# The second feed-forward's three products as Strassen block products, on one core of a Trainium2

## The chip, the cores and the metric

The kernel runs on one core of a Trainium2 chip. The core has five engines with instruction queues of their own: PE (TensorE, matrix products), DVE (VectorE), ACT (ScalarE), POOL (GpSimd) and SP, which here issues all DMAs. PE writes its results to PSUM, which has eight banks of 512 float32 columns in 128 partitions; all else lies in SBUF, and the inputs, outputs and scratch of the kernel in DRAM. The metric is the device time of one execution in microseconds (us).

## The reference

Attention over 4 sequences of 576 tokens with 8 heads gives 2304 tokens of width 512. Two feed-forwards follow; the change is in the second.

```python
def _moe_ref(x, w_in, w_out):            # 512 -> 2048 -> 512
    h = x @ w_in
    g = h * np.cos(h)
    return (g @ w_out).astype(np.float32)

def _moe2_ref(x, w1, w2, w3, w_out):     # 512 -> 768 -> 512
    h = np.maximum(np.maximum(x @ w1, x @ w2), x @ w3)
    return (h @ w_out).astype(np.float32)
```

The weights of both feed-forwards arrive as 8-byte floats.

## The kernel before

The tokens stand in the free dimension and the features in the partitions. Each float32 operand is split into a high and a low half of type float32r, and a product is three matmuls (`PASSES`: high by high, low by high, high by low), each with a 128 by 128 stationary weight and up to 512 token columns. Tokens go in blocks of 512, 512, 512, 512 and 256.

The weights pass four steps: a DMA of the 8-byte words (`w_load`), a correction of the exponent on ACT (`w_exponent`, L177), two integer instructions on DVE that make the float32 bits (`w_bits`, L183 and L186), and the two halves (`w_halves`: L140 on ACT or DVE for the high one, L196 on POOL or DVE for the low one).

The first part of the program does the attention of the first block. Then come 80 steps of the first feed-forward, 16 for each block. A step has 12 matmuls of the first product (L346, inside `h_chunks`), 12 of the second (L389, inside `acc_chunk`), the chain for h cos h on DVE and ACT (L362 or L360, L366, L369, L205, L378, and then the halves L140 or L136 and L380), and a share of the next block's attention. The product alternates between two PSUM banks, so the matmuls of step s + 2 wait until L378 of step s has read its bank. The block's result goes through DRAM (`x1d`).

The second feed-forward has 30 steps (`ff2_h`, `ff2_acc`), 6 for each block. A step has three products of 12 matmuls (L346), of which DVE keeps the running maximum (L434, then L436 twice, each reading one PSUM bank), the halves of the maximum (L438 on ACT, L439 on DVE) and 12 matmuls of the output product (L389). Its tokens come back from `x1d` through `x1_raw` and are split again into a ring of 1536 columns (`x1_split`, L418 on ACT and L419 on DVE). Its 24 weight tiles of 128 by 512 are loaded and made ready in the last steps of the first feed-forward and the first ones of the second.

The Python order is not the engines' order. The tile layer places the instructions on each engine by costs of its own, and adds the semaphore waits; what it has placed is executed strictly in that order on each engine. Buffers are named tags of pools with a fixed number of copies, and a copy is free again when its last reader is done.

## Time and profile before

| | |
|---|---|
| median of 3 runs | 849.5 us (849.34 to 851.74) |
| profiled execution | 849.88 us, of which the span from first to last instruction 848.1 us |
| mean granted TensorE clock | 0.978 of full speed |
| busy share: PE, weight loads, DVE, ACT, POOL | 96%, 78%, 63%, 40%, 13% |
| second feed-forward, first to last matmul | 548.5 to 844.4 us |

A line of code names an instruction in the profile: L346 is the matmul of the hidden products of both feed-forwards, L389 that of both output products. "Busy" is the share of time in which an engine executed; a busy PE in this table is a stream of matmuls, not a peak rate. What to read first is how long PE runs without a gap, and in which stretches the other engines have time left.

### The profile page before, as it was taken

The page shows a single profiled execution, that of the slowest core. Times are in us where ns is not written, and L with a number is a line of the kernel's source. Part 1 is how long each engine was busy: PE and PEld are TensorE (multiplying, and loading weights), DVE is VectorE, ACT ScalarE, POOL GpSimd, SP SyncE. Part 2 cuts the span into 40 slices and gives each one's busy share as a digit, 9 for nine tenths or more (in the row PEclk, how much of TensorE's full clock was granted, in tenths as well). Part 3 has the DMA queues.
Part 4 walks back from the last instruction along what each step waited for, and adds up shares of the span by engine and source line. Part 5 has one row for each costly group of instructions (what it writes and reads, how often), then busy time and mean ns, then how long its engine had stood idle before and what let it go on. Part 6 is the DMA issues. An engine that isn't in the chain of part 4 may idle for free.

```text
span 848.1 us, 11770 instructions
## 1 busy us (share of the span) xinstructions
PE 816.0 (96%) x4358; PEld 659.8 (78%) x4358; DVE 530.3 (63%) x1376; ACT 341.7 (40%) x770; POOL 107.9 (13%) x96
## 2 busy tenths in 40 slices
PE   7858899999999999999999999999999999999998
PEld 6635677777777877777878889888888888888898
DVE  5888979658776678877665589995242242232232
ACT  5777877537663267673331246500020020010010
POOL 1454535310000000000000001230000000000000
PEclk9976989999999999999999999999999999999999
DMA  9953111102111021112200049400030020010010
GB/s 352 417 217 154 32 49 50 49 17 84 49 42 41 1 82 35 48 47 66 71 14 1 1 141 362 180 1 0 1 100 1 0 87 1 1 62 1 1 50 26
DMA packets 23818, 62.22 MB, mean 73 GB/s; under 512 B 2640, under 2 KB 4304, under 8 KB 23760
## 3 DMA queue, kind: packets, MB, share of 16 engines
q1 hardware_dynamic: 23760, 61.47, 20.6%
q8 instruction: 34, 0.56, 0.3%
q14 instruction: 24, 0.20, 0.1%
HBM read 52.02 MB, written 9.44 MB: 72 GB/s over the span
## 4 chain that ended last, share of the span: by engine, by line
PE 83%; DVE 7%; DMA 6%; issue 1%; ACT 1%; SPq 1%; POOL 0%; POOLq 0%; ACTq 0%
PE bank L346 47%; PE bank L389 30%; PE bank L256 3%; DMA w<-in_w_in 3%; PE bank L314 2%; DMA w<-in_w_out 2%; PE bank L303 1%; DVE wx L186 1%; DVE wx L183 1%; DVE r L369 1%; DVE gt L380 1%; DVE r L366 1%; DVE r L378 1%; DMA w<-in_w 1%; DVE e L263 0%
## 5 line engine op out<-in xcount | busy, mean ns | idle before, releaser
L346 PE MATMUL bank<-ring,w 128*128 128x512 f32 (+1 forms) x2040 | 465.4, 376 | 9.4 <-DVE r L378 7.1
L346 PEld LDWEIGHTS bank<-ring,w 128*128 128x128 f32 x2040 | 354.0, 190 | 78.1 <-DVE r L378 8.4
L389 PE MATMUL bank<-gt,w 128*128 128x512 f32 (+1 forms) x1320 | 303.5, 375 | 0.5 <-DVE gt L380 0.5
L389 PEld LDWEIGHTS bank<-gt,w 128*128 128x128 f32 x1320 | 229.6, 190 | 45.7 <-DVE gt L380 0.7
L438 ACT CAST gt<-mx 128x512 fp32r<-128x512 f32 (+1 forms) x30 | 17.3, 578 | 221.2 <-DVE mx L436 221.2
L205 ACT ACT_TABLE_LOAD x62 | 79.5, 1283 | 54.6 <-DVE r L369 45.8
L205 ACT ACTIVATE r<-r,hpi 128x512 f32<-128x512 f32 (+1 forms) x80 | 54.5, 681 | 114.6 <-DVE r L369 114.0
L436 DVE TENSOR_TENSOR mx<-bank,mx 128x512 f32<-128x512 f32 (+1 forms) x60 | 38.2, 637 | 88.5 <-PE bank L346 88.4
L205 ACT ACTIVATE e<-e,m 96x128 f32<-96x128 f32 x192 | 74.8, 391 | 7.1 <-DVE m L263 6.6
L196 POOL TENSOR_TENSOR w<-wx,w 128x512 fp32r<-128x512 f32 x44 | 63.4, 1447 | 111.7 <-ACT w L140 39.8
L378 DVE TENSOR_TENSOR r<-bank,r 128x512 f32<-128x512 f32 (+1 forms) x80 | 50.4, 631 | 22.2 <-ACT r L205 22.0
L434 DVE COPY mx<-bank 128x512 f32<-128x512 f32 (+1 forms) x30 | 19.1, 636 | 70.0 <-PE bank L346 70.0
L263 DVE CUSTOM_DVE_ANT_0 e<-bank,cs 96x128 f32<-96x128 f32 x192 | 45.1, 282 | 24.0 <-PE bank L256 11.8
L362 DVE TENSOR_SCALAR kk<-bank 128x512 int32<-128x512 f32 (+1 forms) x64 | 39.7, 621 | 28.7 <-PE bank L346 28.7
L366 DVE SCALAR_TENSOR_TENSOR r<-kk,bank 128x512 f32<-128x512 int32 (+1 forms) x80 | 50.3, 629 | 8.2 <-ACT kk L360 7.1
L136 POOL TENSOR_SCALAR gt<-r 128x512 fp32r<-128x512 f32 x24 | 15.2, 632 | 290.4 <-PE bank L389 238.0
L380 DVE TENSOR_TENSOR gt<-r,gt 128x512 fp32r<-128x512 f32 (+1 forms) x65 | 42.7, 658 | 13.5 <-POOL gt L136 10.3
L186 DVE SCALAR_TENSOR_TENSOR wx<-w,wx 128x512 int32<-128x512 int32 x56 | 44.8, 801 | 0.4
L256 PEld LDWEIGHTS bank<-qkv 64*96 64x96 f32 x288 | 24.2, 169 | 21.2 <-issue 9.5
L369 DVE TENSOR_SCALAR r<-r 128x512 f32<-128x512 f32 (+1 forms) x80 | 37.7, 471 | 0.9
L256 PE MATMUL bank<-qkv 64*96 64x128 f32 x288 | 34.7, 303 | 3.5 <-DVE m L263 2.6
L177 ACT ACTIVATE w<-w 128x512 f32<-128x512 f32 x56 | 36.2, 672 | 2.5 <-DMA w<-in_w_o 1.1
(37 smaller groups left out, 507.2 us busy)
## 6 DMA issues: line engine op xcount, KB each, us to landing
qkv<-in_qkv SPq DMA_DIRECT2D x36, 336.0 KB, 2.9
w<-in_w SPq DMA_DIRECT2D x18, 512.0 KB, 4.9
w<-in_w_in SPq DMA_DIRECT2D x16, 512.0 KB, 9.3
w<-in_w_out SPq DMA_DIRECT2D x16, 512.0 KB, 9.8
qkv<-in_qkv SPq DMA_DIRECT2D x12, 432.0 KB, 9.2
x1d<-o SPq DMA_DIRECT2D x16, 256.0 KB, 2.5
x1raw<-x1d SPq DMA_DIRECT2D x16, 256.0 KB, 2.8
outT<-o SPq DMA_DIRECT2D x16, 256.0 KB, 2.0
```

Of the source, the lines that this page charges most:

```text
L186: nc.vector.scalar_tensor_tensor(out=x, in0=low, scalar=29, in1=x, op0=ALU.logical_shift_right, op1=ALU.bitwise_or)
L196: tensor("w_lo").tensor_tensor(out=w[:, 1, :], in0=x, in1=w[:, 0, :].bitcast(F32), op=ALU.subtract)
L205: last_table.append(nc.scalar.activation(*args, **kw).ins)
L256: nc.tensor.matmul(sv, q[rows], k[rows], start=True, stop=True)
L263: nc.vector.tensor_tensor_reduce(out=e[:, 2 * j + h, :], in0=places_of[j, h], in1=mask[:, kind, :], scale=-1.0 / math.sqrt(D), scalar=3e38 ...
L346: nc.tensor.matmul(hv, w[:, a, 128 * c : 128 * c + 128], ring[c][:, x, c0 : c0 + n_tok], start=n == 0 and j == 0, stop=n == NC - 1 and j == 2,
L362: nc.vector.tensor_scalar(out=kk.bitcast(I32), in0=hv, scalar1=INV2PI, scalar2=0.25, op0=ALU.mult, op1=ALU.add)
L366: nc.vector.scalar_tensor_tensor(out=r, in0=kk.bitcast(I32), scalar=-2.0 * math.pi, in1=hv, op0=ALU.mult, op1=ALU.add)
L369: nc.vector.tensor_scalar(out=r, in0=r, scalar1=ARG_HI, scalar2=ARG_LO, op0=ALU.min, op1=ALU.max)
L378: nc.vector.tensor_tensor(out=r, in0=hv, in1=r, op=ALU.mult)
L380: tensor("g_lo").tensor_tensor(out=gt[:, 1, :], in0=r, in1=gt[:, 0, :].bitcast(F32), op=ALU.subtract)
L389: nc.tensor.matmul(a_dm, w[:, a, 128 * dm : 128 * dm + 128], gt[:, x, :], start=first and n == 0, stop=last and n == 2,)
```

## The change

The second feed-forward goes in three blocks of 768 tokens. Each of the three weight matrices is cut into three groups of 256 features, which makes nine "quads" for a block, numbered by feature group f and matrix j = 0, 1, 2. In a quad the 512 by 256 weight is a 2 by 2 matrix A of 256 by 256 blocks (feature half, input half), and the tokens are a 2 by 2 matrix B (input half, token half of 384). The four blocks of the result are made by Strassen's seven products in Winograd's form. A product is 2 chunks by 3 passes, 6 matmuls of 384 columns.

Four sums of A blocks (S1 to S4) are made on DVE for each quad and block (`a_sums`); A11, A12, A22 and the sums are then split, high half on ACT, low half on POOL (`a_direct`, `a_split`, `a_22`). Four sums of B blocks (T1 to T4) and the halves of B11, B21, B22 and the Ts are made once for each block on DVE and ACT (`b_make`). Four of the products are added in PSUM to an earlier one (`first` is False in `SUMS`); of three partial sums a copy is taken to SBUF on ACT between two products (`take`), and DVE adds the rest while it reads PSUM (`put`), and then takes the maximum over j, in SBUF.

The weights are no longer made ready in place. During the first feed-forward, 48 half tiles of 128 by 256 go through the DMA load, the exponent and the bits, and are stored as float32 in DRAM (`raw_piece`, `wd` and `wod`). Each quad of each block loads its 512 KB from `wd` again (`raw_load`). The output weights are loaded and split once, on ACT and DVE. The attention's inputs have 4 buffers instead of 5 (`RUNS`).

```diff
-AT2 = [RING - TB, 0, TB, RING - TB, 0]
+HALF = 384
+NB2 = NT // (2 * HALF)
+NQUAD = 3 * NF2 // 2
 LAG = 3
-RUNS = 5
...
+    cv = pool("cv", 2)
...
+    wd = drp.tile([NQUAD, 128, 2, 512], F32, name="wd")
+    wod = drp.tile([NF2 // 2, 128, 2, 512], F32, name="wod")
...
+        (dst[:, 256 * k : 256 * k + 256], w[:, 256 * k : 256 * k + 256]) for dst, w in halves2 for k in range(2)
+    ]
+    pieces2 = {}
+    def raw_piece(n):
+        if 0 <= n - 2 < len(halves2):
+            x = cv.tile([128, 256], I32, tag="c", name="cv")
+            bits(x, pieces2.pop(n - 2))
+            nc.sync.dma_start(out=halves2[n - 2][0], in_=x.bitcast(F32))
+        if 0 <= n - 1 < len(halves2):
+            exponent(pieces2[n - 1])
+        if 0 <= n < len(halves2):
+            w = wx.tile([128, 256], I64, tag="x", name="wh")
+            nc.sync.dma_start(out=w, in_=halves2[n][1])
+            pieces2[n] = w
...
+    QUADS = [(f, j) for f in range(NF2 // 2) for j in range(3)]
+    SUMS = {
+        1: ("X", "A11", "B11", True),
+        5: ("V", "S1", "T1", True),
+        2: ("Y", "A12", "B21", True),
+        6: ("X", "S2", "T2", False),
+        3: ("V", "S4", "B22", False),
+        7: ("X", "S3", "T3", False),
+        4: ("X", "A22", "T4", False),
+    }
...
+    def split(out, x, lo):
+        nc.scalar.copy(out[:, 0], x)
+        lo.tensor_tensor(out=out[:, 1], in0=x, in1=out[:, 0].bitcast(F32), op=ALU.subtract)
+    def raw_load(q):
+        if q < NB2 * NQUAD:
+            raws[q] = slot_tile(q % 3, [128, 2, 512], F32, "raw")
+            nc.sync.dma_start(out=raws[q], in_=wd[q % NQUAD])
+    def a_direct(q):
+        if q < NB2 * NQUAD:
+            ops[q] = {}
+            w = slot_tile(3 + q % 2 * 3, [128, 2, 512], F32R, "wa")
+            split(w, raws[q][:, 0], nc.gpsimd)
+            ops[q]["A11"], ops[q]["A12"] = w[:, :, :256], w[:, :, 256:]
+    def a_22(q):
+        if q < NB2 * NQUAD:
+            w = wx.tile([128, 2, 256], F32R, tag="x", name="w22")
+            split(w, raws.pop(q)[:, 1, 256:], nc.gpsimd)
+            ops[q]["A22"] = w
+    sums = {}
...
+                    sums[q] = slot_tile(9, [128, 4, 256], F32, "ws")
+                else:
+                    sums[q] = gp.tile([128, 4, 256], F32, tag="g", name="ws")
+                do = ((0, a21, a22, ALU.add), (1, sums[q][:, 0], a11, ALU.subtract))
+            else:
+                do = ((2, a11, a21, ALU.subtract), (3, a12, sums[q][:, 1], ALU.subtract))
+            for k, x, y, op in do:
+                nc.vector.tensor_tensor(out=sums[q][:, k], in0=x, in1=y, op=op)
...
+            w = slot_tile(4 + n + q % 2 * 3, [128, 2, 512], F32R, "wa")
+            x = sums[q].rearrange("p a n -> p (a n)")[:, 512 * n : 512 * n + 512]
+            split(w, x, nc.gpsimd)
+            for k in range(2):
...
+        split(wo[f], raws["o"][:, f % 2], nc.vector)
+    braw = {}
...
+        of = {"T1": ("B12", "B11"), "T2": ("B22", "T1"), "T3": ("B22", "B12"), "T4": ("B21", "T2")}
+        for name in names:
+            if name in of:
+                x, y = of[name]
+                out = keep or sp.tile([128, HALF], F32, tag="e", name="bt")
+                nc.vector.tensor_tensor(out=out, in0=braw[x], in1=braw[y], op=ALU.subtract)
+                braw[name] = out
+            if keep is None:
+                split(b_op(name, c), braw[name], nc.vector)
+    bank_of = lambda q: {"X": bank[4 + q % 2], "V": bank[6], "Y": bank[7]}
...
+        to, a, b, first = SUMS[p]
+        out = bank_of(q)[to][:, :HALF]
+        for c in range(2):
+            for n, (x, y) in enumerate(PASSES):
+                nc.tensor.matmul(
+                    out,
+                    ops[q][a][:, x, 128 * c : 128 * c + 128],
+                    b_op(b, c)[:, y],
+                    start=first and c == 0 and n == 0,
+                    stop=c == 1 and n == 2,
+                    skip_group_check=not first,
+                )
+    taken = {}
+    mx = {}
...
+        x = tmp.tile([128, HALF], F32, tag="r", name=name)
+        nc.scalar.copy(x, bank_of(q)[to][:, :HALF])
...
+        f, j = QUADS[q % NQUAD]
+        x = bank_of(q)[to][:, :HALF]
+        if j == 0 and (f, r) not in mx:
+            mx[f, r] = slot_tile(10 + f % 2 * 2 + r, [128, 2, HALF], F32, "mx")
+        m = mx[f, r][:, n]
+        if name is None:
             if j == 0:
-                m = tmp.tile([128, TB], F32, tag="r", name="mx")[:, : BLOCKS[t]]
-                nc.vector.tensor_copy(m, hv)
+                nc.scalar.copy(m, x)
             else:
-                nc.vector.tensor_tensor(out=m, in0=hv, in1=m, op=ALU.max)
-        gt = gp.tile([128, 2, TB], F32R, tag="g", name="gt")[:, :, : BLOCKS[t]]
-        nc.scalar.copy(gt[:, 0, :], m)
-        nc.vector.tensor_tensor(
-            out=gt[:, 1, :], in0=m, in1=gt[:, 0, :].bitcast(F32), op=ALU.subtract
-        )
-        g[s] = gt
-    def ff2_acc(s):
-        t, f = divmod(s, NF2)
-        for dm in range(NC):
-            acc_chunk(outT, STARTS[t], f == 0, f == NF2 - 1, halves[("o", f)], g[s], dm)
+                nc.vector.tensor_tensor(out=m, in0=x, in1=m, op=ALU.max)
+        else:
+            y = taken.pop((q, name))
+            o = m if j == 0 else y
+            nc.vector.tensor_tensor(out=o, in0=y, in1=x, op=ALU.add)
+            if j:
+                nc.vector.tensor_tensor(out=m, in0=m, in1=y, op=ALU.max)
+        if j == 2:
+            g = slot_tile(14 + f * 4 + r * 2 + n, [128, 2, HALF], F32R, "g2")
+            split(g, m, nc.vector)
+            g2[f, r, n] = g
+            if (r, n) == (1, 0):
+                del mx[f, 0], mx[f, 1]
...
+        a = acc[(2 * dm + n) % 4][:, :HALF]
+        for r in range(2):
+            for k, (x, y) in enumerate(PASSES):
+                nc.tensor.matmul(
+                    a,
+                    wo[2 * f + r][:, x, 128 * dm : 128 * dm + 128],
+                    g2[f, r, n][:, y],
+                    start=f == 0 and r == 0 and k == 0,
+                    stop=f == NF2 // 2 - 1 and r == 1 and k == 2,
...
+            accs = [(acc2, t, *x) for x in ACCS]
+            first = t * NQUAD
+            for p in (1, 5, 2):
+                product(first, p)
+                post(first, p)
+            for q in range(first, first + NQUAD):
+                then = q + 1 if q + 1 < first + NQUAD else None
+                for p in (6, 3, -1, 7, -5, -2, 4):
+                    if p > 0:
+                        product(q, p)
+                        post(q, p)
+                    elif then is None:
+                        do, *x = accs.pop(0)
+                        do(*x)
+                    else:
+                        product(then, -p)
+                        post(then, -p)
+                    if p == 6:
+                        if q:
+                            a_22(q + 1)
+                        a_direct(q + 2)
+                        a_sums(q + 2, 0)
+                    if p == 3:
+                        raw_load(q + 3)
+                    if p == -1:
+                        a_sums(q + 2, 1)
+                        a_split(q + 2, 0)
+                    if p == -2:
+                        a_split(q + 2, 1)
+                    if p == 7 and 0 < q <= NF2:
+                        o_weights(q - 1)
+                    if p == 7 and q == first + NQUAD - 2 and t + 1 < NB2:
+                        b_load(t + 1, 0)
+            for n, (do, *x) in enumerate(accs):
+                do(*x)
+                if t + 1 < NB2:
+                    if n == 8:
+                        b_load(t + 1, 1)
+                    for c in range(2):
+                        k = n - 1 - 10 * c
+                        if k in (0, 2, 4, 6):
+                            b_make(c, (("B11", "T1"), ("B21", "T2"), ("B22", "T3"), ("T4",))[k // 2])
...
+            if j == 5:
+                raw_piece(s - NF1)
         for u in us:
             to_exp.append(u)
...
```

In the matmul stream of the second feed-forward, this is one step before: two products on banks 4 and 5 (98 and 99), the output product on banks 0 to 3 (94 to 97). A row ends with the number of like instructions in it.

```order
L346 MATMUL bank_99<-ring_145,w 128x512 x3
L346 MATMUL bank_99<-ring_146,w 128x512 x3
L346 MATMUL bank_99<-ring_147,w 128x512 x3
L346 MATMUL bank_99<-ring_148,w 128x512 x3
L389 MATMUL bank_94<-gt,w 128x512 x3
L389 MATMUL bank_95<-gt,w 128x512 x3
L389 MATMUL bank_96<-gt,w 128x512 x3
L389 MATMUL bank_97<-gt,w 128x512 x3
```

And this is PE in the changed kernel, in a quad of the first block, two rows for a product: 3, the next quad's 1, 7, the next quad's 5 and 2, and 4. Bank 101 is X of the next quad, 102 X of this one, 103 is V, 104 is Y.

```order
L560 MATMUL bank_103<-ring_152,wa 128x384 x3
L560 MATMUL bank_103<-ring_153,wa 128x384 x3
L560 MATMUL bank_101<-ring_150,wa 128x384 x3
L560 MATMUL bank_101<-ring_151,wa 128x384 x3
L560 MATMUL bank_102<-ring_150,wa 128x384 x3
L560 MATMUL bank_102<-ring_151,wa 128x384 x3
L560 MATMUL bank_103<-ring_150,wa 128x384 x3
L560 MATMUL bank_103<-ring_151,wa 128x384 x3
L560 MATMUL bank_104<-ring_152,wa 128x384 x3
L560 MATMUL bank_104<-ring_153,wa 128x384 x3
L560 MATMUL bank_102<-ring_152,w_5104 128x384 x3
L560 MATMUL bank_102<-ring_153,w_5104 128x384 x3
```

The products of two quads are interleaved, so that between two uses of one bank there are two or more other products; the output product is no longer between them but at the end of a block.

On DVE in the second feed-forward of the kernel before, between two steps (with buffer numbers; bank4 to bank7 are PSUM):

```order
L439 TENSOR_TENSOR gt_5593<-mx_5565,gt_5593 128x512
L434 COPY mx_5622<-bank6_100 128x512
L436 TENSOR_TENSOR mx_5622<-bank7_101,mx_5622 128x512
L436 TENSOR_TENSOR mx_5622<-bank4_98,mx_5622 128x512
L439 TENSOR_TENSOR gt_5650<-mx_5622,gt_5650 128x512
```

On DVE in the changed kernel, from the end of a quad with j = 2 in the first block to the start of one with j = 0; `ws` are the S sums of a later quad, `raw` its weights, `g2` the halves of the maximum.

```order
L594 TENSOR_TENSOR s2_5663<-s2_5663,bank6_103 128x384
L596 TENSOR_TENSOR mx_5484<-mx_5484,s2_5663 128x384
L474 TENSOR_TENSOR g2_5682<-mx_5484,g2_5682 128x384
L594 TENSOR_TENSOR v5_5634<-v5_5634,bank5_102 128x384
L596 TENSOR_TENSOR mx_5544<-mx_5544,v5_5634 128x384
L509 TENSOR_TENSOR ws_5835<-raw_5769 128x256 x2
L474 TENSOR_TENSOR g2_5708<-mx_5544,g2_5708 128x384
L594 TENSOR_TENSOR mx_5730<-s1_5693,bank7_104 128x384
L509 TENSOR_TENSOR ws_5835<-ws_5835,raw_5769 128x256
L590 TENSOR_TENSOR mx_5544<-bank5_102,mx_5544 128x384
L509 TENSOR_TENSOR ws_5835<-raw_5769,ws_5835 128x256
L474 TENSOR_TENSOR g2_5742<-mx_5544,g2_5742 128x384
```

Instructions that read PSUM (L590, L594) now alternate with ones whose two inputs are both in SBUF (L474, L509, L596), and POOL has four of its own in each quad.

On DVE in the first feed-forward, one step of the second block before (chain for h cos h, and the low half of g):

```order
L378 TENSOR_TENSOR r_2542<-bank4_98,r_2542 128x512
L380 TENSOR_TENSOR gt_2530<-r_2508,gt_2530 128x512
L362 TENSOR_SCALAR kk_2574<-bank5_99 128x512
L366 SCALAR_TENSOR_TENSOR r_2576<-kk_2574,bank5_99 128x512
L369 TENSOR_SCALAR r_2576<-r_2576 128x512
```

And in the changed kernel, a step of the same block (`cv` and `wh` are a half tile of the weights; L389 there is L378 before, L391 is L380, L373, L377 and L380 are L362, L366 and L369):

```order
L389 TENSOR_TENSOR r_2627<-bank4_101,r_2627 128x512
L391 TENSOR_TENSOR gt_2615<-r_2586,gt_2615 128x512
L187 TENSOR_SCALAR cv_3779<-wh_3702 128x256
L190 SCALAR_TENSOR_TENSOR cv_3779<-wh_3702,cv_3779 128x256
L373 TENSOR_SCALAR kk_2666<-bank5_102 128x512
L187 TENSOR_SCALAR cv_3830<-wh_3743 128x256
L377 SCALAR_TENSOR_TENSOR r_2668<-kk_2666,bank5_102 128x512
L190 SCALAR_TENSOR_TENSOR cv_3830<-wh_3743,cv_3830 128x256
L380 TENSOR_SCALAR r_2668<-r_2668 128x512
```

Two half tiles stand between the instructions of this step; over the whole first feed-forward the 48 pairs are placed between steps 12 and 41 of 80.

## Rows read from the trace of the kernel before

**Rows 1.** The page: busy us, share of the span and instructions of each engine.

```profile
PE 816.0 (96%) x4358; PEld 659.8 (78%) x4358; DVE 530.3 (63%) x1376; ACT 341.7 (40%) x770; POOL 107.9 (13%) x96
```

**Rows 2.** Timeline of PE, start of the second feed-forward (start, us, engine, line).

```profile
548.48 16.51 PE L346 MATMUL bank<-ring,w 128*128 128x512 f32 x72
...
567.55 8.32 PE L346 MATMUL bank<-ring,w 128*128 128x512 f32 x36
...
578.43 1.75 PE L346 MATMUL bank<-ring,w 128*128 128x512 f32 x7
```

**Rows 3.** Timeline of PE, the last block of 256 tokens.

```profile
819.72 4.48 PE L346 MATMUL bank<-ring,w 128*128 128x256 f32 x36
...
825.48 4.48 PE L346 MATMUL bank<-ring,w 128*128 128x256 f32 x36
...
841.32 3.08 PE L389 MATMUL bank<-gt,w 128*128 128x256 f32 x24
```

**Rows 4.** Busy us by stretch: PE, PEld, DVE, ACT, POOL, granted clock, DMA share, GB/s.

```profile
200.00:220.00 20.00, 20.00 (x113) 14.76 (x112) 16.83 (x64) 14.17 (x34) 0.62 (x1) 1.00 0.26 77
320.00:340.00 20.00, 20.00 (x120) 14.88 (x117) 16.87 (x61) 14.07 (x34) 0.84 (x2) 1.00 0.16 42
520.00:540.00 20.00, 19.33 (x157) 18.73 (x156) 20.00 (x52) 12.88 (x26) 3.25 (x2) 1.00 0.93 342
540.00:560.00 20.00, 19.46 (x117) 17.29 (x116) 19.91 (x42) 5.70 (x13) 4.72 (x4) 1.00 0.08 28
560.00:600.00 40.00, 40.00 (x179) 33.11 (x178) 26.12 (x42) 2.48 (x4) 6.56 (x4) 1.00 0.00 1
```

**Rows 5.** Groups by line and shape: busy us, mean ns of one, idle before.

```profile
L436 DVE TENSOR_TENSOR mx<-bank,mx 128x512 f32<-128x512 f32 x48 | 33.1, 690 | 76.3 <-PE bank L346 76.2
L436 DVE TENSOR_TENSOR mx<-bank,mx 128x256 f32<-128x256 f32 x12 | 5.1, 425 | 12.2 <-PE bank L346 12.2
L438 ACT CAST gt<-mx 128x512 fp32r<-128x512 f32 x24 | 14.9, 621 | 188.7 <-DVE mx L436 188.7
```

**Rows 6.** Timeline of DVE: three instructions back to back (start, us).

```profile
502.10 0.42 DVE L362 TENSOR_SCALAR kk<-bank 128x256 int32<-128x256 f32 x1
502.44 0.68 DVE L186 SCALAR_TENSOR_TENSOR wx<-w,wx 128x512 int32<-128x512 int32 x1
503.04 0.41 DVE L366 SCALAR_TENSOR_TENSOR r<-kk,bank 128x256 f32<-128x256 int32 x1
```

**Rows 7.** Timelines of POOL and of DVE, the same moments.

```profile
525.61 1.46 POOL L196 TENSOR_TENSOR w<-wx,w 128x512 fp32r<-128x512 f32 x1 [6.38 <-DMA w<-in_w]
...
525.83 1.52 DVE L380 TENSOR_TENSOR gt<-r,gt 128x256 fp32r<-128x256 f32 x1
...
509.28 1.30 POOL L196 TENSOR_TENSOR w<-wx,w 128x512 fp32r<-128x512 f32 x1 [8.08 <-ACT r L205]
...
509.30 0.41 DVE L378 TENSOR_TENSOR r<-bank,r 128x256 f32<-128x256 f32 x1
...
559.62 3.07 POOL L196 TENSOR_TENSOR w<-wx,w 128x512 fp32r<-128x512 f32 x1 [2.99 <-PE bank L346]
...
559.65 0.67 DVE L419 TENSOR_TENSOR ring<-x1raw,ring 128x512 fp32r<-128x512 f32 x1
560.25 0.67 DVE L439 TENSOR_TENSOR gt<-mx,gt 128x512 fp32r<-128x512 f32 x1
560.85 0.68 DVE L186 SCALAR_TENSOR_TENSOR wx<-w,wx 128x512 int32<-128x512 int32 x1
```

**Rows 8.** DMA time from issue to landing, 18 loads from `in_w`, 512 KB each.

```profile
DMA to landing us min/median/max: 3.6/4.9/5.6
```

**Rows 9.** Timelines of PE and of DVE: one PSUM bank in the first feed-forward.

```profile
339.47 0.85 PE L346 MATMUL bank<-ring,w 128*128 128x512 f32 x3
...
346.87 0.85 PE L346 MATMUL bank<-ring,w 128*128 128x512 f32 x3
...
341.51 0.68 DVE L378 TENSOR_TENSOR r<-bank,r 128x512 f32<-128x512 f32 x1
```

More of the change, by code (lines that the diff above doesn't have):

```diff
@@ L188, in w_bits, with w_exponent @@
         )
+    def w_exponent(key):
+        exponent(words[key])
+    def w_bits(key):
+        x = wx.tile([128, 512], I32, tag="x", name="wx")
+        bits(x, words[key])
         words[key] = x.bitcast(F32)
@@ L383, in ff1_g, with acc_chunk @@
         g[s] = gt
-    def acc_chunk(dst, t0, first, last, w, gt, dm):
+    def acc_chunk(t0, first, last, w, gt, dm):
         n_tok = gt.shape[-1]
@@ L421, in body @@
-    flip = [0]
-    def ff2_h(s):
-        t, f = divmod(s, NF2)
-        m = None
-        for j in range(3):
-            hv = (h_bank + a_bank)[flip[0] % 4][:, : BLOCKS[t]]
-            flip[0] += 1
-            chunk = h_chunks(hv, halves[(j, f)], AT2[t], BLOCKS[t])
-            for n in range(NC):
-                chunk(n, n)
+            nc.sync.dma_start(out=x1d[dm, :, t0 : t0 + n_tok], in_=o)
+    halves2 = [(wd[f // 2 * 3 + k, :, f % 2], w123[k, f]) for f in range(NF2) for k in range(3)]
@@ new lines, in body @@
+    halves2 += [(wod[f // 2, :, f % 2], w_o2[f]) for f in range(NF2)]
+    halves2 = [
+        (dst[:, 256 * k : 256 * k + 256], w[:, 256 * k : 256 * k + 256]) for dst, w in halves2 for k in range(2)
[12 more added lines that the diff above has]
+            pieces2[n] = w
@@ new lines, in put, with post @@
+        if j == 2:
[4 more added lines that the diff above has]
+                del mx[f, 0], mx[f, 1]
+    def post(q, p):
+        if p == 1:
+            take(q, "s1", "X")
+        if p == 5:
+            take(q, "v5", "V")
+        if p == 2:
+            put(q, 0, 0, "s1", "Y")
+        if p == 6:
+            take(q, "s2", "X")
+        if p == 3:
+            put(q, 0, 1, "s2", "V")
+        if p == 7:
+            put(q, 1, 1, "v5", "X")
+        if p == 4:
+            put(q, 1, 0, None, "X")
@@ new lines, in body, with ff2_early @@
+    ACCS = [(dm, n, f) for d in (0, 2) for fs in ((0, 1), (2,)) for dm in (d, d + 1) for n in range(2) for f in fs]
+    late = []
+    def ff2_early(k):
+        if k in (1, 2, 3):
+            raw_load(k - 1)
+        if k in (0, 8):
+            b_load(0, k // 8)
+        c, n = divmod(k - 2, 8)
+        if k >= 2 and n < 6 and c < 2:
+            if n == 5:
+                late.append(slot_tile(12 + c, [128, HALF], F32, "bt3"))
+                b_make(c, ("T3",), keep=late[c])
+            else:
+                b_make(c, (("B11", "T1"), ("B21",), ("T2",), ("B22",), ("T4",))[n])
+        if k == NF1:
+            for c in range(2):
+                split(b_op("T3", c), late[c], nc.vector)
+        q, n = divmod(k - 7, 4)
+        if q in (0, 1):
+            if n == 0:
+                a_direct(q)
+                a_sums(q, 0)
+            if n == 1:
+                a_sums(q, 1)
+                a_split(q, 0)
+            if n == 2:
+                a_split(q, 1)
+                a_22(q)
```

117 lines of the change are left out of this document (66 added, 51 removed).

## Prediction

> **What bounds the kernel now.** The page's first part gives PE 96% of the span and no other engine over 63% [rows 1]; that alone does not say that PE sets the pace, because a stream of matmuls is drawn as busy whatever its rate. The timeline of PE says it. In the second feed-forward 36 matmuls of the hidden products and 12 of the output product start again every 578.43 - 567.55 = 10.88 us [rows 2], 226.7 ns for each matmul of 512 columns, and in the last block every 825.48 - 819.72 = 5.76 us [rows 3], 120.0 ns for 256 columns. Both without a gap, since 24 steps of 10.88 and 6 of 5.76 make 295.7 us, and the stretch from 548.48 to 841.32 + 3.08 = 844.40 is 295.9 us. The two pitches lie on a line of 106.7 ns for 256 columns and 13.3 ns beside it. So this third of the program costs its matmul columns and nothing else; the table by stretch shows DVE, ACT and POOL with time to spare from 560 us on [rows 4]. Before it PE is full as well, with DVE close behind: 16.8 of 20 us in two stretches of the first feed-forward, and all of 520 to 560 us, the only place there where PE lost time (0.67 and 0.54 us) [rows 4].
>
> **The matmuls.** Removed: 295.9 us. Added, for each of three blocks: 9 quads of 7 products and 24 output groups (4 output chunks, 2 token halves, 3 feature groups), each 6 matmuls of 384 columns: 3 x 87 x 6 = 1566. A width of 384 is not in the trace; halfway between the two pitches it is 173.3 ns, and the bounds are 120.0 and 226.7. The line has no reason to bend between them, so I take 173.3: 271.4 us. That is 24.5 us less. The output product has the same columns as before and pays only for more, shorter matmuls. With 849.88 - 295.9 = 554.0 us for all else, the sum so far is 825.4 us. The profiled execution is 0.4 us above the median of the runs, which I leave out.
>
> **The work that must stay hidden: DVE and POOL.** Seven products take 7 x 6 x 173.3 ns = 7.28 us, and in that time a quad needs, on POOL, three low halves of 512 columns at 1.30 us [rows 7] and one of 256 (no row: between half and the whole of 1.30; I take 0.70, near the half), 4.6 us together. On DVE it needs four sums of 256 columns; for j = 1 and 2 three maxima of 384 in SBUF; for j = 2 also four low halves of 384; and three or four reads of PSUM of 384. For 384 columns I go between 425 and 690 ns, 557 ns for one alone [rows 5]; in a run the starts are 0.34 us apart at 256 and 0.60 at 512 [rows 6], so 0.47 at 384. That is at most 15 instructions in a quad, 1.36 + 1.41 + 1.88 + 4 x 0.47 = 6.5 us for j = 2. Each engine alone fits into 7.28 us. ACT too: in three quads 10 copies and 16 high halves, at 512 columns or fewer and so no longer than 0.62 us [rows 5], 16 of 21.84 us.
>
> But DVE and POOL do not run side by side. At 525.83 a DVE instruction of 256 columns with both inputs in SBUF took 1.52 us instead of the 0.42 of [rows 6], and ended just after the POOL instruction that had begun before it; at 509.30 one that reads PSUM ran inside a POOL instruction and took 0.41. At 559.62 it was POOL that waited, 3.07 us instead of 1.30, while three DVE instructions with two SBUF inputs followed each other [rows 7]. So low halves on POOL and sums, maxima and low halves on DVE take turns.
>
> Taking turns, a quad needs 4.6 + 1.36 = 5.96 us for j = 0, 5.96 + 1.41 = 7.37 for j = 1 and 7.37 + 1.88 = 9.25 for j = 2: 22.6 us for three quads against 21.84 on PE. What is queued behind a blocked DVE instruction is the next read of PSUM; PE waits for it two products later (product 4 needs the X bank that DVE read after product 7, the next quad's 5 needs V after 3), 2.08 us. Lower bound of the loss: nothing, if that slack covers every turn. Upper bound: the 11 reads of PSUM on DVE in three quads never lie beside POOL, 22.6 + 11 x 0.47 = 27.8, 5.9 us a triple, 53 us over nine. If the spare time of j = 0 is all used, a triple loses 0.75 us; if none is, because sums can be made only two quads ahead, the excess of j = 2, 2.0 us. I take the middle, 1.4 us, nine times: 12.6 us. The Trainium skill puts this as a rule in SBUF — State Buffer, Who interferes with whom: VectorE and GpSimd share one port pair, a VectorE instruction with two SBUF inputs contends with a GpSimd one that reads SBUF, and the later one blocks until the first is done. By that rule each waits for one instruction, and the loss above would be its lower figure, 0.75 us a triple or 835 us in all; the row at 559.62, where POOL let three pass, makes for the higher one.
>
> **Block ends.** For each block, DVE makes 8 Ts and 14 low halves of B, 22 x 0.47 = 10.3 us. For the second and third block 21 output groups of 1.04 us, 21.8 us, lie behind the last quad and hide them, except for some ten that stand among the last quad's own instructions: I take 1 us for each of the two ends (0 to 4.7), 2 us. The 24 output groups need no POOL.
>
> **The first feed-forward.** 48 half tiles of two integer instructions, each at most 0.34 us [rows 6], are up to 33 us of DVE between steps 12 and 41. In the fullest stretches DVE has 3.1 of 20 us left [rows 4], 1.17 us in a step of 346.87 - 339.47 = 7.4 us, and gets one or two half tiles, 0.68 to 1.36. PE's tolerance: L378 ended at 341.51 + 0.68 = 342.19, and the matmuls that reuse its bank began at 346.87 [rows 9], 4.7 us later. So the first 4.7 us that DVE falls behind cost nothing. Behind the added instructions on DVE's queue stand that same chain and the attention's. Bounds: 0, and 8 us (140 us of full stretches are 19 steps, 19 us added against 11 if half of the spare time can't be used in order). I take 2. On ACT 48 exponents of about 0.4 us lie in stretches with 6 of 20 us free. On SP's queue the loads and stores stand between the loads of the attention's inputs; these are asked for four units ahead instead of five, some 30 us at one unit a step, so a store that waits for DVE for a step delays nothing. From 490 us on the bits of the 24 tiles go away, and B and S preparation for the first block (10.3 + 8 x 0.34 + 6 x 0.60 = 16.6 us) comes: a little less on DVE where PE lost 1.2 us, of which I give back 1. Net of this part: 1 us.
>
> **The loads of each quad.** The slot is free when POOL is done with A22, 1.6 us after product 4 (-1.04 + 0.62 + 1.30 + 0.70 from the end of the next quad's 2). Landing takes 3.6 us at the least in the trace, 4.9 in the median, 5.6 at most [rows 8], the longer ones at 342 GB/s [rows 4]; here 512 KB in 7.28 us are 72 GB/s. 1.6 + 3.6 = 5.2, and DVE asks for the data after the next product 7 and its low half on POOL, 4.16 + 0.62 + 1.30 = 6.1 us. I take nothing; at 5.6 us it would be 1.1 us late.
>
> The sum: 825.4 + 12.6 + 2 + 1 = 841.0 us.
>
> **Rivals.** First, the turns cost nothing: PE stays dense as in the old second feed-forward, 825 to 833 us. For it: every use of a bank has at least two products between, and the order spreads the POOL work. Against it: the j = 2 quad is 2 us too long in any order.
> Second, slower than before: DVE and POOL set the pace of each quad, with the PSUM reads stuck behind blocked instructions. Place: product 4 and the next quad's 5 wait for DVE in each quad. From (24.5 - 3) / 9 = 2.4 us a triple on the gain is gone; at 5.9 us it is 825.4 + 53 + 3 = 881 us. For it: DVE can't step over a blocked instruction [rows 7]; against it: POOL's four instructions leave 2.7 of 7.28 us, and j = 0 needs little.
> Third, the loads land late: 1.1 us in 27 quads, 30 us, 841 + 30 less what overlaps with the turns, 850 to 865 us. Against it: the light traffic.
> Fourth, the change does not bring what it says because a matmul of 384 columns takes as long as one of 512: 1566 x 226.7 ns are 355 us, and the time is 909 us without any turn. Against it: 256 columns at 120.0 ns, with a weight load for each matmul [rows 3]. Excluded but for 1 in 100.
>
> **How the numbers follow.** What can be told from no change here is 0.3%, 847 to 852 us. The forecast with its own range of 833 to 847 us has 0.50; the dense case 0.24, all of it faster; the second rival 0.15, of it 0.02 within 0.3%; the third and a first feed-forward that falls behind by 8 us 0.10, of it 0.06 within 0.3%; the fourth 0.01. Faster 0.74, same 0.08, slower 0.18. The range takes in the dense sum and reaches up until about 0.12 is left above and 0.05 below: 825 to 857 us.
>
> **What would show it.** Matmuls at 173 ns when none waits. POOL and DVE instructions with SBUF inputs drawn at two to four times their length, most in the j = 2 quads, and PE idle before L560 with DVE as its releaser, under a microsecond at a time, about 1.4 us every third quad. No wait of DVE for the loads, the start of the second feed-forward within 2 us of 548.5. Wrong if PE has no gaps (first rival), waits in every quad (second), DVE waits for the `wd` loads (third), or the first feed-forward ends more than 5 us late.

## The result, and the profile after

The changed kernel takes 856.6 us (median of 4, 856.1 to 858.23) against 849.42 before: ratio 1.0083, interval [1.0059, 1.0108]: 0.8% slower, more than the 0.3% that the prediction takes for no change. The profiled execution took 856.1 us.

The page's first part, beside [rows 1]: PE is busy for less time, DVE for 106 us more.

```profile
PE 798.4 (93%) x4484; PEld 678.7 (79%) x4484; DVE 636.0 (74%) x1619; ACT 454.4 (53%) x1028; POOL 221.3 (26%) x192
```

The timeline of PE in the second feed-forward, beside [rows 2]: one triple of quads, from 572.42 to 597.32.

```profile
553.19 0.70 PE L560 MATMUL bank<-ring,wa 128*128 128x384 f32 x3
553.73 1.69 PE L400 MATMUL bank<-gt,w 128*128 128x256 f32 x12
555.25 9.01 PE L560 MATMUL bank<-ring,wa 128*128 128x384 f32 x51
...
572.42 2.24 PE L560 MATMUL bank<-ring,wa 128*128 128x384 f32 x12
575.89 4.43 PE L560 MATMUL bank<-ring,wa 128*128 128x384 f32 x24 [1.23 <-DVE mx L590]
580.26 1.33 PE L560 MATMUL bank<-ring,w 128*128 128x384 f32 x6
581.43 2.25 PE L560 MATMUL bank<-ring,wa 128*128 128x384 f32 x12
584.70 4.46 PE L560 MATMUL bank<-ring,wa 128*128 128x384 f32 x24 [1.02 <-DVE mx L590]
589.00 1.20 PE L560 MATMUL bank<-ring,w 128*128 128x384 f32 x6
590.03 6.40 PE L560 MATMUL bank<-ring,wa 128*128 128x384 f32 x36
...
627.07 1.34 PE L560 MATMUL bank<-ring,wa 128*128 128x384 f32 x6 [1.58 <-ACT s L576]
...
631.71 1.34 PE L560 MATMUL bank<-ring,w 128*128 128x384 f32 x6 [1.23 <-DVE v L594]
...
828.29 22.00 PE L625 MATMUL bank<-g,w 128*128 128x384 f32 x126
```

Where PE doesn't wait, 36 matmuls of 384 columns take 596.27 - 590.03 = 6.24 us, 173.3 ns each. But a triple takes 597.32 - 572.42 = 24.9 us instead of 21.84. After two quads of three, PE stands before the next quad's product 1: its bank X was last used by product 4, two products earlier, and DVE's read of that (L590) is late. The second feed-forward ends at 850.29 and takes 295.6 us, as before (295.9), when the 1.5 us of L400 in its beginning are taken off; its gain of 24.5 us is gone in stalls. The slowdown itself is ahead of it: the first feed-forward ends 6.2 us later (555.25 - 0.54 - 548.48).

DVE, POOL and PE around one late read, beside [rows 7] (start, us; idle before and releaser in brackets):

```profile
595.15 1.54 POOL L474 TENSOR_TENSOR wa<-ws,wa 128x512 fp32r<-128x512 f32 x1 [1.27 <-ACT wa L473]
596.72 0.76 DVE L509 TENSOR_TENSOR ws<-raw 128x256 f32<-128x256 f32 x2 [1.18 <-POOL wa L474]
597.22 1.42 POOL L474 TENSOR_TENSOR wa<-raw,wa 128x512 fp32r<-128x512 f32 x1 [0.53 <-ACT wa L473]
597.32 2.25 PE L560 MATMUL bank<-ring,wa 128*128 128x384 f32 x12
597.40 1.52 DVE L509 TENSOR_TENSOR ws<-ws,raw 128x256 f32<-128x256 f32 x1
598.84 0.54 DVE L594 TENSOR_TENSOR s<-s,bank 128x384 f32<-128x384 f32 x1
599.31 0.49 DVE L509 TENSOR_TENSOR ws<-raw,ws 128x256 f32<-128x256 f32 x1
599.72 0.55 DVE L596 TENSOR_TENSOR mx<-mx,s 128x384 f32<-128x384 f32 x1
600.19 0.54 DVE L590 TENSOR_TENSOR mx<-bank,mx 128x384 f32<-128x384 f32 x1
600.78 4.46 PE L560 MATMUL bank<-ring,wa 128*128 128x384 f32 x24 [1.23 <-DVE mx L590]
```

DVE first waits 1.18 us for POOL to finish with a sums buffer, then one sum of 256 columns lasts 1.52 us beside a POOL instruction of 1.42, and only behind those comes the read.

Groups by line, second feed-forward, beside [rows 5] (busy, mean ns, idle before): maxima in SBUF take 959 ns, reads of PSUM of the same size 546.

```profile
L474 POOL TENSOR_TENSOR wa<-raw,wa 128x512 fp32r<-128x512 f32 x25 | 35.1, 1402 | 94.1 <-ACT wa L473 94.1
L596 DVE TENSOR_TENSOR mx<-mx,s 128x384 f32<-128x384 f32 x36 | 34.5, 959 | 0.6
L474 POOL TENSOR_TENSOR w<-raw,w 128x256 fp32r<-128x256 f32 x25 | 22.2, 887 | 6.4 <-ACT w L473 6.4
L590 DVE TENSOR_TENSOR mx<-bank,mx 128x384 f32<-128x384 f32 x18 | 9.8, 546 | 0.6 <-PE bank L560 0.6
```

The quads' loads, beside [rows 8] (KB, median us to landing), come in time:

```profile
raw<-wd SPq DMA_DIRECT2D x27, 512.0 KB, 3.3
```

### The profile page after: what moved, and what is told of

Same layout as the page of the kernel before. It is cut to its first block, busy times and chain, and to the rows that moved or that the text cites. A ratio compares the mean times of both kernels' runs of the same rounds, so it can differ in the third digit from the quotient of the medians.

```text
span 854.3 us, 13038 instructions
## 1 busy us (share of the span) xinstructions
PE 798.4 (93%) x4484; PEld 678.7 (79%) x4484; DVE 636.0 (74%) x1619; ACT 454.4 (53%) x1028; POOL 221.3 (26%) x192
## 4 chain that ended last, share of the span: by engine, by line
PE 59%; DVE 16%; DMA 11%; issue 5%; POOL 4%; ACT 3%; SPq 1%; POOLq 0%; ACTq 0%; DVEq 0%
PE bank L400 17%; PE bank L357 16%; PE bank L560 11%; PE bank L625 8%; DMA wh<-in_w 4%; DVE ws L509 3%; DMA w<-in_w_in 3%; PE bank L267 3%; POOL wa L474 2%; DMA w<-in_w_out 2%; PE bank L325 2%; DVE mx L596 2%; PE bank L314 1%; DVE r L377 1%; DVE s L594 1%
## 5 line engine op out<-in xcount | busy, mean ns | idle before, releaser
L357 PE MATMUL bank<-ring,w 128*128 128x512 f32 (+1 forms) x960 | 236.0, 385 | 12.4 <-DVE r L389 10.3
L400 PE MATMUL bank<-gt,w 128*128 128x512 f32 (+1 forms) x960 | 224.4, 376 | 0.0
L357 PEld LDWEIGHTS bank<-ring,w 128*128 128x128 f32 x960 | 167.6, 193 | 47.0 <-DVE r L389 11.5
L560 PE MATMUL bank<-ring,wa 128*128 128x384 f32 x972 | 177.2, 336 | 15.7 <-DVE mx L590 12.5
L400 PEld LDWEIGHTS bank<-gt,w 128*128 128x128 f32 x960 | 164.9, 189 | 33.6
L560 PEld LDWEIGHTS bank<-ring,wa 128*128 128x128 f32 x972 | 168.4, 188 | 20.1 <-DVE mx L590 16.3
L474 POOL TENSOR_TENSOR wa<-ws,wa 128x512 fp32r<-128x512 f32 x54 | 74.0, 1372 | 66.4 <-ACT wa L473 65.1
L625 PE MATMUL bank<-g,w 128*128 128x384 f32 x432 | 76.3, 334 | 0.0
L625 PEld LDWEIGHTS bank<-g,w 128*128 128x128 f32 x432 | 75.0, 188 | 0.0
L389 DVE TENSOR_TENSOR r<-bank,r 128x512 f32<-128x512 f32 (+1 forms) x80 | 50.4, 632 | 20.4 <-ACT r L216 20.4
L474 POOL TENSOR_TENSOR wa<-raw,wa 128x512 fp32r<-128x512 f32 x27 | 37.6, 1394 | 102.3 <-ACT wa L473 98.5
L373 DVE TENSOR_SCALAR kk<-bank 128x512 int32<-128x512 f32 (+1 forms) x64 | 39.8, 621 | 21.5 <-PE bank L357 20.8
L377 DVE SCALAR_TENSOR_TENSOR r<-kk,bank 128x512 f32<-128x512 int32 (+1 forms) x80 | 50.3, 629 | 4.1 <-ACT kk L371 2.6
L391 DVE TENSOR_TENSOR gt<-r,gt 128x512 fp32r<-128x512 f32 (+1 forms) x65 | 40.4, 621 | 13.6 <-POOL gt L139 10.3
L267 PEld LDWEIGHTS bank<-qkv 64*96 64x96 f32 x288 | 24.5, 164 | 24.1 <-issue 8.0
```

Of the source, the lines that this page charges most:

```text
L267: nc.tensor.matmul(sv, q[rows], k[rows], start=True, stop=True)
L357: nc.tensor.matmul(hv, w[:, a, 128 * c : 128 * c + 128], ring[c][:, x, c0 : c0 + n_tok], start=n == 0 and j == 0, stop=n == NC - 1 and j == 2,
L377: nc.vector.scalar_tensor_tensor(out=r, in0=kk.bitcast(I32), scalar=-2.0 * math.pi, in1=hv, op0=ALU.mult, op1=ALU.add)
L389: nc.vector.tensor_tensor(out=r, in0=hv, in1=r, op=ALU.mult)
L391: tensor("g_lo").tensor_tensor(out=gt[:, 1, :], in0=r, in1=gt[:, 0, :].bitcast(F32), op=ALU.subtract)
L400: nc.tensor.matmul(a_dm, w[:, a, 128 * dm : 128 * dm + 128], gt[:, x, :], start=first and n == 0, stop=last and n == 2,)
```

## The experiments

### What makes the second feed-forward wait

**More banks for X (e1_x4).**

```diff
-    bank_of = lambda q: {"X": bank[4 + q % 2], "V": bank[6], "Y": bank[7]}
+    bank_of = lambda q: {"X": bank[(4, 5, 2, 3)[q % NQUAD % 4]], "V": bank[6], "Y": bank[7]}
```

> The sums X of a quad go over four PSUM banks in place of two, so that a bank comes again after four quads, not two. Theory A (the distance): DVE's read of X after product 4 is late by up to 1.2 us now and then, because it stands behind blocked instructions, but DVE and POOL have time over three quads. Then PE's two waits per triple for L590 go, 3.06 us a triple becomes under 0.5, and the time falls by 18 to 24 us, to 832 to 838. Theory B (the pace): DVE and POOL together need more than 21.84 us for three quads. Then PE waits elsewhere, for V, Y or the operands, and the time stays within 853 to 859.

855.65 us, 1.0079 [1.0063, 1.0095]. The waits for L590 are gone, but PE now waits 11.5 us for ACT's copies of partial sums and 5.5 us for L594, and a triple takes 24.7 us. Theory A falls. PE's groups in the second feed-forward:

```profile
L560 PE MATMUL bank<-ring,wa 128*128 128x384 f32 x972 | 177.0, 336 | 11.5 <-ACT s L576 11.5
L560 PE MATMUL bank<-ring,w 128*128 128x384 f32 x162 | 33.4, 340 | 5.5 <-DVE v L594 5.5
```

**The low halves of A on DVE (e2_lo_on_dve).**

```diff
-            split(w, raws[q][:, 0], nc.gpsimd)
+            split(w, raws[q][:, 0], nc.vector)
```

(and the same in `a_22` and `a_split`)

> All low halves of A on DVE, none on POOL, so nothing takes turns. By the starts in a run DVE then needs 20.4 us of the 21.84 of three quads. Theory A, with the turns as the cause of the late reads: the waits shrink to below 1 us a triple, 838 to 848. Theory B: the pace is then DVE's alone, 20.4 us, below PE's, so also 838 to 848. If the order on DVE's queue is what makes the reads late, without any turn: the queue has 4 instructions more per quad ahead of the reads, the waits grow, 860 to 875.

829.8 us, 0.9777 [0.9761, 0.9792]: faster than before, and better than any theory gave. PE has no stall in the whole second feed-forward:

```profile
551.63 0.71 PE L560 MATMUL bank<-ring,wa 128*128 128x384 f32 x3
...
570.87 6.40 PE L560 MATMUL bank<-ring,wa 128*128 128x384 f32 x36
577.11 1.20 PE L560 MATMUL bank<-ring,w 128*128 128x384 f32 x6
578.15 6.40 PE L560 MATMUL bank<-ring,wa 128*128 128x384 f32 x36
```

It runs from 551.63 to 802.91 + 22.00 = 824.91, 273.3 us; less the 1.5 us of L400 that is 271.8, where the prediction's dense sum was 271.4.

**No low halves in blocks 2 and 3 (e3_no_lo).**

```diff
-        lo.tensor_tensor(out=out[:, 1], in0=x, in1=out[:, 0].bitcast(F32), op=ALU.subtract)
+        if not skip:
+            lo.tensor_tensor(out=out[:, 1], in0=x, in1=out[:, 0].bitcast(F32), op=ALU.subtract)
...
-                    ops[q][a][:, x, 128 * c : 128 * c + 128],
+                    ops[q][a][:, x if q < NQUAD else 0, 128 * c : 128 * c + 128],
```

(`skip` is `q >= NQUAD`, blocks 2 and 3.)

> Leaves out the low halves of A in the second and third block (the products use the high half twice), so POOL has nothing there; DVE's and ACT's work and all matmuls stay. If POOL is the cause, by turns or by what waits for it: blocks 2 and 3 dense, 91 us each instead of about 98, and 840 to 844 in all. If DVE's own queue or ACT's copies are: no change, 855 to 857.

838.22 us, 0.988 [0.9861, 0.9899]; block 2 takes 744.05 - 653.57 = 90.5 us instead of 100.0. POOL is the cause, by whichever way.

**POOL works, but nobody waits for it (e5_pool_alone).**

```diff
+        if skip:
...
+            a, b = (idle[0][:, k, :n] for k in range(2))
+            nc.gpsimd.tensor_tensor(out=a, in0=b, in1=out[:, 0].bitcast(F32), op=ALU.subtract)
```

> As the run without low halves in blocks 2 and 3 (the products use the high half twice), but POOL does an instruction of the same size at each of those places, as soon as ACT's high half is there: it subtracts that from a constant tile, into a scrap tile that nobody reads. So POOL has the same work, DVE and PE never wait for it, and only the sharing of SBUF between POOL and DVE is left. Theory A (taking turns is the whole loss): each of the two blocks loses its 8 us again, a triple takes 24 to 25 us, and 852 to 857 in all. Theory B (the loss is DVE's wait for POOL's result, for the sums' buffers and so on): both blocks stay at 91 us, 838 to 841.

849.46 us, 0.9998 [0.9982, 1.0014], between the theories. A triple takes 693.83 - 670.16 = 23.67 us: sharing SBUF costs 1.8 of the 3.05 us; the rest goes with the waits for POOL's results, which this run leaves out.

**A third buffer for the sums (e6_third_buffer).**

```diff
-                if q < 2:
+                if q < 2 or q % 3 == 1:
                     sums[q] = slot_tile(9, [128, 4, 256], F32, "ws")
```

> The sums S have three buffers in place of two, so DVE's sums need not wait until POOL has split the sums of two quads before (20 us of DVE's idle time end so). Theory A (turns set the pace): DVE gets there sooner and takes its turn sooner, the total of the turns is the same, 852 to 858. Theory B (the buffer): the waits of PE shrink by half or more, 838 to 846.

863.95 us, 1.0154 [1.0115, 1.0193]: slower still, and outside both ranges. DVE hardly waits for the buffer any more (2.4 us for 19.2), but the sums now wait for the loads and meet POOL ahead of the same read; PE's longest waits for that read grow to 1.9 us and the first triple takes 597.47 - 571.45 = 26.0 us.

**The sums queued behind the reads (e13_sums_behind).**

```diff
-                nc.vector.tensor_tensor(out=sums[q][:, k], in0=x, in1=y, op=op)
+                with tc.issue_after(reads[-1]) if reads else nullcontext():
+                    nc.vector.tensor_tensor(out=sums[q][:, k], in0=x, in1=y, op=op)
```

(`reads` collects the instructions of L590 and L594 as the program makes them.)

> The low halves are on POOL as in the changed kernel; each sum S is queued on DVE behind the PSUM read that stands last before it in the program, so the read of X after product 4 no longer stands behind four sums that wait for POOL. Theory A1 (the order): PE's waits for that read fall to under 0.4 us each, a triple takes 22 to 23 us and not 24.9, 836 to 846. Theory A2 (the pace of DVE and POOL together): the wait moves to the operands or to other reads, a triple stays at 24.5 to 25.5 us, 853 to 860.

857.57 us, 1.0092 [1.0071, 1.0113]. The read of X is nearly on time now (waits of 0.3 us at most), and PE waits for others instead, 6.8 us for reads of V and 5.0 for ACT's copies; a triple takes 705.50 - 681.05 = 24.45 us. Neither banks, buffers nor order help.

**Only the sums' low halves on DVE (e9_half_lo)**, the edit of e2 in `a_split` alone.

> Only the low halves of the sums S go to DVE; those of A11, A12 and A22 stay on POOL. Taking turns sets the pace: in three quads POOL's 3 x (1.40 + 0.92) = 7.0 us and DVE's two-input work, 8.8 + 6 x 0.60 = 12.4 us, make 19.4 us, and with the 1.7 us by which the present kernel's 24.9 exceed the same sum (14.4 + 8.8 = 23.2) 21.1 us, just under the 21.84 of PE: dense or nearly so, 830 to 836. If each POOL instruction costs PE something wherever it lies, half of them is still on POOL and half of the 24 us stays: 841 to 845.

842.77 us, 0.9927 [0.9905, 0.9949]: in the second range, though the profiled execution, 839.16, is in neither. A triple takes 22.59 us, where my sum of 21.1 would have left PE dense at 21.84. Two POOL instructions in a row still sit ahead of the read of X.

One triple of block 2 in each of these, by the table by stretch (stretch, its us, then busy us and instructions of PE, PEld, DVE, ACT, POOL, granted clock, DMA share, GB/s). No low halves:

```profile
664.00:685.81 21.81, 21.81 (x127) 21.81 (x126) 15.09 (x34) 12.86 (x26) 0.00 (x0) 1.00 0.22 74
```

All low halves on DVE:

```profile
667.59:689.55 21.96, 21.96 (x127) 21.81 (x127) 20.75 (x46) 12.84 (x27) 0.00 (x0) 1.00 0.22 72
```

Half of them on POOL:

```profile
664.81:687.40 22.59, 22.39 (x127) 21.76 (x127) 21.65 (x40) 12.72 (x26) 6.96 (x7) 1.00 0.22 70
```

POOL working for nobody:

```profile
670.16:693.83 23.67, 22.94 (x128) 21.70 (x127) 20.40 (x34) 12.63 (x26) 14.90 (x12) 1.00 0.21 67
```

The changed kernel:

```profile
672.41:697.30 24.89, 22.63 (x127) 21.76 (x127) 20.23 (x34) 12.65 (x26) 14.99 (x13) 1.00 0.20 64
```

Sums behind the reads:

```profile
681.05:705.50 24.45, 23.34 (x127) 21.68 (x127) 23.42 (x34) 12.36 (x27) 15.61 (x13) 1.00 0.20 65
```

The column to read is DVE's, with the same 34 instructions in four of the rows: 15.09 us when POOL is silent, 20.2 to 23.4 when POOL does the low halves, and 20.75 when DVE does them itself, in 12 more instructions. POOL's help takes as much of DVE's time as the work is worth, and adds waits. In the last row DVE is busy 96% of the triple and has next to no time left.

The maxima in SBUF say the same one by one. They take 959 ns in the changed kernel; in block 2, with POOL silent and with POOL working for nobody:

```profile
L597 DVE TENSOR_TENSOR mx<-mx,s 128x384 f32<-128x384 f32 x12 | 6.7, 557 | 0.3
```

```profile
L606 DVE TENSOR_TENSOR mx<-mx,s 128x384 f32<-128x384 f32 x12 | 9.9, 821 | 0.3
```

### What delays the first feed-forward

Its end is read at the first L560: 548.48 before (L346 there), 553.19 after. The expectations name that row or the main stream two microseconds behind it. Each start is that of one execution, and executions of one kernel differ by some microseconds (821.11 to 827.03 in e8), so the medians stand beside it.

**Zeros stored instead of the float32 bits (e4_zero_store on the changed kernel, e10_zero_on_dve on e2).**

```diff
-            bits(x, pieces2.pop(n - 2))
-            nc.sync.dma_start(out=halves2[n - 2][0], in_=x.bitcast(F32))
+            pieces2.pop(n - 2)
+            nc.sync.dma_start(out=halves2[n - 2][0], in_=zero)
...
-            exponent(pieces2[n - 1])
```

> Leaves out the exponents and the bits of the 48 half tiles; the loads and stores stay, but zeros are stored. If DVE's and ACT's added instructions hold up the first feed-forward: the second one starts at 548 to 550 us instead of 555, and 849 to 852 in all. If it is the DMAs, the four buffers instead of five, or the new order in the first block: it starts at 553 or later, 854 to 857 in all.

858.27 us, 1.0107 [1.0078, 1.0136], above both ranges. Its profiled execution took 2642.36 us, so no trace of it is used.

> With all low halves on DVE (829.8 us): leaves out the exponents and bits of the 48 half tiles and stores zeros; the 96 DMAs stay. Theory C (DVE's added instructions crowd the attention steps of the first feed-forward): near the run without any staging, 820 to 823, second feed-forward from 543 us. Theory D (the DMAs, or the place on the queue): 828 to 831, from 552 us.

829.72 us, 0.9759 [0.9738, 0.9779]: no gain on e2 by the medians; the start at 547.66 is that of an execution of 827.05 us, the shortest of the four. Inconclusive, because PE has one wait of 5.3 us (L314 for DVE's L306) that no other run has. Ahead of L306 on DVE's queue stands a copy of a result, L410, which waits 5.75 us for an earlier store to `x1d`, and that store stands on SP's queue behind seven loads of half tiles:

```profile
188.78 9.27 SPq L436 DMA_DIRECT2D wh<-in_w  x7
198.10 0.91 SPq L413 DMA_DIRECT2D x1d<-o  x2
```

With no bits to wait for, the 48 loads are issued from 147 to 224 us, in e2 from 149 to 354.

**No staging (e7_no_staging), and five input buffers again (e8_no_staging_runs5).**

```diff
-            nc.sync.dma_start(out=raws[q], in_=wd[q % NQUAD])
+            nc.sync.dma_start(out=raws[q], in_=x1d[:2, :, :512].rearrange("k p n -> p k n"))
...
-                raw_piece(s - NF1)
+                pass
```

> With all low halves on DVE (829.8 us), and the 48 half tiles left out altogether: no load, exponent, bits or store. The loads of each quad take 512 KB from the first feed-forward's result instead, of the same shape. If the staging, in whatever part, delays the second feed-forward: it starts at 548 to 549 us instead of 553.7, and 824 to 826 in all. If it doesn't: 828 to 831.

820.29 us, 0.9651 [0.9624, 0.9678], from 540.91: with low halves on DVE the staging costs 10.7 us by the starts (551.63 - 540.91) and 9.5 by the medians (829.8 - 820.29).

> As the run without staging, and the attention's inputs have five buffers again. If the four buffers delay the first feed-forward: 2 us or more less than without staging alone, a start of the second one at 548 to 549 us. If not: the same as that run within 1 us.

822.61 us, 0.9676 [0.964, 0.9712]: no faster, so the four buffers cost nothing.

**The arithmetic without the DMAs (e14_bits_no_dma).**

```diff
-            bits(x, pieces2.pop(n - 2))
-            nc.sync.dma_start(out=halves2[n - 2][0], in_=x.bitcast(F32))
+            bits(x, one[0])
...
-            exponent(pieces2[n - 1])
+            exponent(one[1])
```

> With all low halves on DVE. The counterpart of the run that stored zeros: all 48 exponents and pairs of bits instructions run, two a step over steps 16 to 41, but on two half tiles loaded once, and nothing is stored (the loads of each quad read the first feed-forward's result). Theory C (the instructions on DVE and ACT): as with the whole staging, 827 to 831, second feed-forward from 550 us on, and the score matmuls of 300 to 400 us again 130 to 140 ns apart. Theory D (the DMAs): as without staging, 819 to 822, from 543 us, 87 ns.

824.48 us, 0.9711 [0.9692, 0.9731], from 545.61: between the two; by the medians 4.2 of the 9.5 us. (It also queues the pairs otherwise than e2: two a step, behind L389.) From the first product of step 16 to that of step 48 it takes 401.38 - 173.82 = 227.6 us, e7 396.62 - 174.81 = 221.8 and e2 407.50 - 175.79 = 231.7. Where its 5.8 us go, the groups by line from 200 to 400 us show, for the attention's score matmuls (busy us, mean ns). Before, and with no staging:

```profile
L256 PE MATMUL bank<-qkv 64*96 64x128 f32 x152 | 17.0, 289 | 0.0
```

```profile
L267 PE MATMUL bank<-qkv 64*96 64x128 f32 x156 | 17.0, 289 | 0.0
```

With the whole staging (e2), and with the arithmetic alone:

```profile
L267 PE MATMUL bank<-qkv 64*96 64x128 f32 x152 | 23.1, 292 | 0.5 <-DVE pt L143 0.5
```

```profile
L267 PE MATMUL bank<-qkv 64*96 64x128 f32 x148 | 22.9, 288 | 0.0
```

With zeros stored it is 16.8 us for 148. One matmul takes nearly the same in all of them; what differs is in how many batches, with no other matmul between, they stand on PE's queue. In the kernel before, a batch of four takes as long as a batch of eight:

```profile
240.86 0.67 PE L256 MATMUL bank<-qkv 64*96 64x128 f32 x4
241.47 0.50 PE L346 MATMUL bank<-ring,w 128*128 128x512 f32 x1
...
249.07 0.68 PE L256 MATMUL bank<-qkv 64*96 64x128 f32 x8
249.68 0.98 PE L346 MATMUL bank<-ring,w 128*128 128x512 f32 x3
```

With the arithmetic alone most batches are of four; with the whole staging (e2) some are of two:

```profile
229.31 0.67 PE L267 MATMUL bank<-qkv 64*96 64x128 f32 x4
...
233.92 0.67 PE L267 MATMUL bank<-qkv 64*96 64x128 f32 x4
```

```profile
208.12 0.46 PE L267 MATMUL bank<-qkv 64*96 64x128 f32 x2
208.50 0.55 PE L314 MATMUL bank<-cs,e 96*128 96x96 f32 x4
208.98 0.46 PE L267 MATMUL bank<-qkv 64*96 64x128 f32 x2
```

From 200 to 400 us PE has 24 such batches before and without staging, 23 with zeros stored, 34 with the arithmetic alone and 37 in e2. So what the added instructions cost here is not time that PE waits for DVE: with them on the queues of DVE and ACT, the tile layer has placed the score matmuls in more and smaller batches, and that order costs the 6 us. Why a batch of four takes as long as one of eight is not shown.

**Spread or moved.** With the bits of each half tile queued behind a step's L389, one a step over steps 16 to 66 (e11_one_a_step), two a step from step 44 (e12_late), or one a step with three buffers for the loads (e15_three_loads):

```diff
-                raw_piece(s - NF1)
+                with tc.issue_after(gate[-1]) if gate else nullcontext():
+                    raw_piece(s - NF1)
```

> With all low halves on DVE, and the bits of each half tile queued on DVE behind the product h cos h of the step before, so that they come one a step over steps 16 to 66 and not one or two a step over 12 to 41. Theory C (crowding): DVE's load in the attention steps halves, 823 to 827. Theory D: 828 to 831.

> The same, with two half tiles a step over steps 44 to 69, where little of the attention is left and DVE has 6 of 20 us free. Theory C: 818 to 823, second feed-forward from 541 to 545 us, unless the first quads' weights come late (then DVE waits for their load at its start). Theory D: 828 to 831.

> As the run with one half tile a step (827.5 us), with three buffers for the loads of the half tiles in place of two (one for what is stored, and one small tile of the softmax less, for room). If ACT's and DVE's waits for late loads are what the staging costs beside its instructions: ACT's 12.3 us of waiting for them fall below 4, and 822 to 825.5, as with the arithmetic alone. If those waits lie in time that ACT has to spare: 826.5 to 829.

827.47 us, 0.9742 [0.9724, 0.9759], the fastest version that computes everything, between its two ranges; 832.59, 0.9798 [0.9783, 0.9813], above both; 828.82, 0.976 [0.9723, 0.9797], in the second. One a step takes away the 11.8 us that DVE in e2 waits for ACT's exponents, and gains 2.3 us; PE still has 35 batches of score matmuls. Late, it has 24 and the scores are as quick as before (17.0 us), but PE waits 10.8 us in all for the reads of the h chain instead of 7.9, another 2.4 us before the output product, and from 500 to 520 us the granted clock is 0.83. The third buffer leaves ACT's waits for loads at 14 us (12.3 with two) and changes nothing. How the rest of the staging's cost comes about, some 4 us in e2 beside the 6 of the score matmuls, stays open.

## Why the prediction was wrong

The forecast was 841.0 us and faster; it is 856.6 and slower. That this lies just inside the range of 825 to 857 us does not bear the sum out: the turns and block ends cost 24.2 us (295.6 - 271.4) for 14.6, the first feed-forward 6.2 for 1.

**Right: the matmuls.** 173.3 ns at 384 columns, and a dense second feed-forward of 271.8 us (e2) for 271.4. **Right: the loads**; DVE never waited for them in the changed kernel.

**Wrong in size: the turns, 12.6 us.** The step that failed is the middle of 1.4 us a triple; it was 3.05, inside the bounds of 0 and 5.9. Two things were missing. POOL's instructions took 14.99 us a triple, not 13.8 (1.36 to 1.40 us at 512 columns, 0.89 for the 256 that I took as 0.70): with that my sum of turns is 23.8 us, and e5, where only turns are left, has 23.67. And POOL was costed as time alone; DVE also waits for its results, and with that a triple takes 24.9 (which of these waits matters is open: e6 took one kind away and gained nothing). The rule of the Trainium skill (SBUF — State Buffer, Who interferes with whom), that the later of the two waits until the first is done, fits the single sum above (1.52 us beside 1.42; 0.42 in e3, where POOL is silent), but my 0.75 us from it rested on the same short POOL times: with the measured ones it is 2.0 us, and e5 lost 1.8.

**Wrong in place.** Not product 4 or 5 but the next quad's product 1 waits, two products after product 4. It is the second rival in two quads of three: from 2.4 us a triple on the gain is gone, and it was 3.05. The slow reads there also make each end of block 1 and 2 cost 1.58 + 1.23 us and two restarts, where I had 1 us.

**Wrong: the first feed-forward, +1 for 6.2 us.** The step that failed is the price of DVE's additions: I measured how long the h chain's bank can wait (4.7 us) and took 2 us for being later than that. The staging cost 10, outside my bounds of 0 and 8, and hardly by lateness: PE's waits for that read are 7.9 us in all with the staging (e2) and 7.9 without it (e7); in the changed kernel they are 10.3, 2.4 of it behind 400 us. The added instructions changed PE's own order, 36 batches of score matmuls for 24 (37 in e2), some 6 us; the other 4 stay open. "PE 20.00 of 20 us" in [rows 4] can't show that. The 6.2 us are what is left after a gain: from the first product of step 16 to that of step 48 the kernel before takes 400.53 - 178.77 = 221.8 us and the changed one 406.16 - 174.22 = 231.9, and the rest of the first feed-forward and the attention ahead of it is 4 us shorter, where I gave back 1. The sum by measured terms is 825.4 + 24.2 + 6.2 = 855.8 us for the 856.1 of the profiled execution.
